# Earlier spectra, later weights: a reordered prologue and a longer pause in an FFT-and-MLP kernel

## The chip, the cores and the metric

The kernel runs on one core of a Trainium2 chip. The metric is the device time of one execution in microseconds (us). The engines are named as in the profile: PE (TensorE, matrix products; PEld its weight loads), DVE (VectorE), ACT (ScalarE), POOL (GpSimd) and SP (SyncE, which here only issues DMA transfers). PEclk is the share of its full clock that TensorE was granted.

## The reference

An input of 8 sequences of 3008 positions by 256 channels goes through a spectral layer and then through a two-layer MLP of 24064 tokens:

```python
X = np.fft.rfft(x, axis=1)                  # x: (8, 3008, 256), 3008 = 47 * 64
Yr = Xr @ w_r - Xi @ w_i + b_r
Yi = Xr @ w_i + Xi @ w_r + b_i
Y = soft_threshold(Yr, 0.01) + 1j * soft_threshold(Yi, 0.01)
y = np.fft.irfft(Y, n=3008, axis=1)
x = y.reshape(8 * 3008, 256)
h = x @ w_in                                # w_in: (256, 2048)
g = np.maximum(0.01 * h, h)
out = g @ w_out                             # w_out: (2048, 256)
```

The MLP's two weight matrices come as float64, so the kernel has to make float32 parts of them itself.

## The kernel before, in words

**Images and stages.** Each of the 8 sequences ("images", b = 0 to 7) passes three stages. `fwd(b)` loads x in pieces of 120 x 512 (`xin`, L235 for b = 0, L238 for later images), folds them on DVE (L245, L246), multiplies by the DFT matrix `fa` on PE (by way of the helper at L78), copies the result from PSUM on ACT (L264) and writes it to a DRAM buffer `u_dram` (L267). `mid(b)` takes the frequencies in 12 pairs of rows j: it reads `u` back (L329), multiplies by the second DFT matrix `fb` (L343), copies and adds (`ef`, L347 and L348), applies the complex weights (`w`), adds the bias part `kc` (L376, L388), soft-thresholds (L391, L392), applies a sign (`zf`, L396 on ACT, L398 and L400), multiplies by `gb`, copies the result `v` (L418) and writes it to `v_dram` (L420). `inverse` reads `v_dram` back and turns it into tokens, and `moe` runs the MLP over 47 chunks of 512 tokens, each product in three float32r terms (high by high, high by low, low by high; L92 into `psh`, L576 into `pso`).

**What overlaps.** Image 0 goes through all its stages first, in plain float32: this is the prologue, some 130 us. From then on PE runs the MLP, and the spectral stages of image b + 1 are laid between its products by `Stream` objects: a stage is a generator that yields its cost, and a stream advances it to a given fraction of its total (`MID` and `FWD`). At the start of `mid(b)` for b > 0 the generator yields a pause of `6 * CS`, right after it has issued the reads of `u` for its first two pairs; the stream spends that share of its total on no instructions.

**Weights in the prologue.** `load_win(c, ...)` loads quarter c of w_in (two halves of 512 KB, L155) and `convert_win(c)` makes its float32 parts: ACT starts with L131 and L132, DVE works on them in L133 to L137 and L162 to L168, then ACT (L171) and DVE (L172) split into high and low parts, twelve DVE instructions in all. `load_weights` loads the spectral weights (L121) and combines them on DVE (L122, L123); `split_consts` splits these and the DFT matrices into high and low parts (ACT L112, DVE L113) for the images after the first. `load_wout` does for w_out, in eight pieces named `raw`, what the former do for w_in; its conversion goes on into the first MLP chunks.

**What sets the order.** Each engine runs its own instructions in a fixed order. A scheduler that is part of the framework chooses this order when the kernel is built, from the order of the code, the data dependences and `tc.issue_after(x)`, which lets nothing under it be issued before x. The lists `written`, `reads`, `turned` and `thresholded` collect instructions of the stages (the writes of `u_dram`, the reads of `u`, the first transforms' copies, the thresholds) for that use. Transfers issued by one engine are issued in that engine's order; a transfer waits for a slot that an earlier one frees.

Of the kernel before, what the change touches and what calls it, by code (L numbers as in the profile page):

```python
# [8 lines left out]
F32 = mybir.dt.float32  # L9
# [9 lines left out]
N1, N2, NK1 = 47, 64, 24  # L19
NG, NS = 5, 13  # L20
P = 128
# [9 lines left out]
def spectral_mlp_kernel(  # L31
# [17 lines left out]
    NB = x.shape[0]  # L49
# [8 lines left out]
    CS = 512  # L58
# [45 lines left out]
    def load_plain(name, src, shape):  # L104
        consts[name] = const.tile(shape, F32, name=name)
        sync.dma_start(consts[name], src)

    def split_consts():
        for name in ("wr", "wd", "wn", "gb", "fa0", "fa1"):
            w = consts[name + "32"][0]  # L110
            hi, lo = pair(name, list(w.shape))
            act.copy(hi, w)  # L112
            dve.tensor_sub(lo, w, hi.bitcast(F32))  # L113
# [32 lines left out]
    def load_win(c, queues, behind=None):  # L146
        if c % 2 == 0:
            tag = ("wout_hi", "wout_lo")[c // 2]
            raw = sb.tile([P, 2, NH * NIN, 2], U32, name="win_raw", tag=tag, bufs=1)
            win_raw.extend((raw[:, 0], raw[:, 1]))  # L150
        r = win_raw[c].rearrange("p (a f) w -> p a (f w)", a=NH)
        iv = w_in.bitcast(U32).rearrange("(a p) f -> p a f", p=P)[:, :, 2 * c * NIN:2 * (c + 1) * NIN]
        for a, q in enumerate(queues):
            with tc.issue_after(behind.ins) if behind is not None else nullcontext():
                q.dma_start(r[:, a], iv[:, a])  # L155
# [19 lines left out]
    def load_wout():  # L175

        n = CS // D
        ov = w_out.bitcast(U32).rearrange("(a p) f -> p a f", p=P)
        raws = []

        def load(early):
            k = len(raws)
            tag, bufs = ("gl", 2) if early else (("e", 1), ("z", 1))[k % 2]
            raw = sb.tile([P, CS, 2], U32, name="raw", tag=tag, bufs=bufs)
            with tc.issue_after(reads[13 if early else -1].ins):
                sync.dma_start(raw.rearrange("p (a f) w -> p a (f w)", a=n), ov[:, k * n:(k + 1) * n, :])
            raws.append(raw)

        for k in range(2):
            load(True)  # L190
        yield 1
        consts["wout"] = tuple(
            sb.tile([P, NF, D], F32R, name=f"wout_{p}", tag=f"wout_{p}", bufs=1) for p in ("hi", "lo"))
        for c in range(NF // n):
            a = sb.tile([P, CS], F32, name="cva", tag="zf", bufs=1)
            q = sb.tile([P, CS], F32, name="cvq", tag="u", bufs=3)
            float64_parts(raws[c], a, q)
            dh, dl = (w[:, c * n:(c + 1) * n, :] for w in consts["wout"])
            a, q = (t.rearrange("p (a f) -> p a f", a=n) for t in (a, q))
            act.copy(dh, a)  # L200
            dve.tensor_sub(a, a, dh.bitcast(F32))
            converted.append(dve.tensor_add(dl, a, q))
            yield 1
            while c >= 1 and len(raws) < min(c + 3, NF // n):
                load(False)
# [2 lines left out]
    u_dram = {}  # L208
    v_dram = {}

    reads, written, turned, turning, thresholded = [], [], [], [], []
    NX = -(-NS // 2)
    XT = [("gf", 2)] + [("gl", 2)] * 2 + [("gh", 2)] * 2 + [("yc", 2)] * 2
    XT1 = [("yc", 2)] * 2 + [("gf", 2), ("gh", 2), ("yl", 2), ("yh", 2), ("gh", 2)]
# [1 line left out]
    def fwd(b):  # L216
# [5 lines left out]
        def load(c):  # L222
            cols = slice(2 * c * D, min(2 * c + 2, NS) * D)
            n = cols.stop - cols.start
            if b < NPRE:
                tag, bufs = (XT, XT1)[b][c]
                x2 = sb.tile([PA, 2, 2 * D], F32, name="xin", tag=tag, bufs=bufs)
                x_t[c] = [x2[:, h, :n] for h in range(2)]
            else:
                x_t[c] = [  # L230
                    sb.tile([PA, 2 * D], F32, name=f"xin{h}", tag="uv"[h], bufs=3 - h)[:, :n] for h in range(2)
                ]
            for h, t in enumerate(x_t[c]):
                if b == 0:
                    (act if h else sync).dma_start(t, x[b, h, :, cols])  # L235
                else:
                    with tc.issue_after(reads[-1].ins):
                        sync.dma_start(t, x[b, h, :, cols])  # L238
# [73 lines left out]
    def mid(b):  # L312
# [49 lines left out]
        def proj(j):  # L362
# [31 lines left out]
            for i in range(2):  # L394
                s = slice(64 * i, 64 * (i + 1))
                act.copy(zf[:64, i, :], t[s, 0, :])  # L396
                if b == 0 and j == NPAIR - 1:
                    dve.tensor_scalar(zf[64:, i, :], t[s, 1, :], sign[s, NK1 + j:NK1 + j + 1], None, ALU.mult)  # L398
                else:
                    act.mul(zf[64:, i, :], t[s, 1, :], sign[s, NK1 + j:NK1 + j + 1])  # L400
            if b == 0:
                z_t[j] = (zf,)
                yield 6 * D
# [8 lines left out]
        def stage_g(j):  # L412
            pg = bank("psh", 4) if b < 1 else bank("psf", 2)
            last = products(pg, [(consts["gb" if b else "gb32"], tuple(flat(z) for z in z_t.pop(j)))])
            if b == 0:
                turning.append(last)
            v = sb.tile([P, 2, D], F32, name="v", tag="v" if b else "y")
            act.copy(flat(v), pg)  # L418
            for c in range(2):
                act.dma_start(vd[c, 2 * j:2 * j + 2, :N2, :].rearrange("k n d -> n k d"), v[c * N2:(c + 1) * N2])  # L420

        for j in range(2):
            load(j)
        yield 6 * CS if b else 0
        if b:
            for s in range(NPAIR):
                if s + 2 < NPAIR:
# [225 lines left out]
    xs3 = sb.tile([PA, 3, 2 * D], F32, name="xs3", tag="yl")  # L653
    f0 = Stream(fwd(0), FWD)
    f0.to(0.01)
    load_win(0, (sync, act))
    load_plain("fb", fb, [P, NK1 + 1, N2])
    load_weights()
    brow = sb.tile([P, 2 * D], F32, name="brow", tag="kb", bufs=1)
    for p in (0, 32):  # L660
        for r, src in enumerate((b_r, b_i)):
            sync.dma_start(brow[p:p + 1, r * D:(r + 1) * D], src.unsqueeze(0))
    sign = const.tile([P, NK1 + NPAIR], F32, name="sign")
    sync.dma_start(sign, sg)
    sync.dma_start(consts["gb32"][0], gb)

    bo = sb.tile([P, 2 * D + P], F32R, name="bz", tag="t", bufs=1)
    bz, ones = bo[:, :2 * D], bo[:, 2 * D:]
    dve.memset(ones.bitcast(F32), 1.0)
    dve.memset(bz.bitcast(F32), 0.0)  # L670
    f0.finish()
    load_win(1, (sync, sync), written[7])
    pair("win", [P, 7, NQ, P])
    win_tmp = (
        sb.tile([P, NH * NIN], F32, name="cva", tag="vin"), sb.tile([P, NH * NIN], F32, name="cvq", tag="gf"),
        sb.tile([P, 4, 2, P], F32, name="ws", tag="yh"))
    act.copy(bz[:1], brow[:1])
    act.copy(bz[32:33], brow[32:33])
    dve.tensor_sub(bz[32:33], brow[32:33], bz[32:33].bitcast(F32))
    act.mul(fa32[:, 2], fa32[:, 1], -1.0)  # L680
    convert_win(0)
    with tc.issue_after(turned[0].ins):
        split_consts()
    m0 = Stream(mid(0), MID)
    m0.to(0.001)
    for c in range(2, 4):
        load_win(c, (sync, sync), reads[3])
    bias = const.tile([P, 2, D], F32, name="bias")
    with tc.issue_after(reads[3].ins):
        load_plain("ga", ga, [PA, 2, P])  # L690
        for r, src in enumerate((b_r, b_i)):
            sync.dma_start(bias[:, r, :], src.unsqueeze(0).broadcast_to([P, D]))
    fp = Stream(fwd(1), FWD)
    with tc.issue_after(turned[0].ins):
        convert_win(1)
    wout = load_wout()
    for i in range(1, 17):
        m0.to(i / 16)
        if i in (3, 8):
            convert_win(2 + i // 8)  # L700
        if 5 <= i < 12:
            next(fp.gen)
        if i == 13:
            next(wout)
# [10 lines left out]
    next(wout)  # L715


    mids = [Stream(mid(b), MID + 6 * CS) for b in range(1, NB)]
    cur, streams = -1, ()
    for i, pos in enumerate(moe()):  # L720
        if i % 2 == 0 and len(converted) < NQ:
# [121 lines left out]
```

## Time and profile before

| what | us |
|---|---|
| runs of the kernel before | 2603.67, 2605.85, 2608.62 |
| median | 2605.85 |
| profiled execution, its own time | 2600.34 |
| span of the profiled execution | 2598.6 |

The profiled execution is one more execution, 5.5 us below the median of the other three; 1.7 us of its time lie outside the span. Mean granted clock over the span: 0.993. In the profile a row of the windows view gives, for a stretch of time, the busy time of each engine with its number of instructions in parentheses. A row of the timeline gives the start, the time, the engine, the line, and the tiles "out<-in"; consecutive like instructions are one row with a count, and what an engine waited for before an instruction stands in brackets. "SPq" and "ACTq" rows are transfers being issued, not being carried out. Engines run side by side, so busy times do not add up to the span.

### The profile page before, as it was taken

How to read it: one execution, taken by the hardware profiler on the slowest of the kernel's cores; microseconds unless marked ns; L12 is line 12 of the kernel's file. 1: busy time of each engine (PE TensorE's matmuls, PEld its weight loads, DVE VectorE, ACT ScalarE, POOL GpSimd, SP SyncE). 2: the span in 40 equal slices, each digit the busy share in tenths (PEclk: the TensorE clock that was granted, in tenths of full speed). 3: DMA queues.
4: the chain of work that ended last, by engine and by line, in shares of the span. 5: the costliest groups of instructions: out<-in, count | busy, mean ns of one | idle time of the engine just before them, and what ended most of it. 6: DMA issues, size and time to landing. Idle time of an engine off the chain costs nothing.

```text
span 2598.6 us, 42643 instructions
## 1 busy us (share of the span) xinstructions
PE 2537.5 (98%) x16300; PEld 2281.5 (88%) x16300; DVE 1897.1 (73%) x3403; ACT 1668.5 (64%) x3174; POOL 229.6 (9%) x180
## 2 busy tenths in 40 slices
PE   5999999999999999999999999999999999999999
PEld 4689888999889998899988999889998889999998
DVE  7687786776777778777786777877777777767675
ACT  5766665776556666567665666566666667655564
POOL 0001121100110001100021000210002000000000
PEclk8999999999999999999999999999999999999999
DMA  8621132111221113211132111321113221101000
GB/s 259 179 85 50 48 89 72 54 47 48 82 78 49 45 41 90 75 55 51 33 97 68 49 49 37 104 67 49 49 36 101 64 58 48 44 17 32 9 17 17
DMA packets 119912, 165.13 MB, mean 64 GB/s; under 512 B 13601, under 2 KB 69917, under 8 KB 119709
## 3 DMA queue, kind: packets, MB, share of 16 engines
q1 hardware_dynamic: 79120, 115.55, 14.6%
q10 hardware_dynamic: 40589, 46.87, 7.1%
q8 instruction: 128, 2.10, 0.4%
q14 instruction: 75, 0.61, 0.1%
HBM read 86.60 MB, written 75.76 MB: 62 GB/s over the span
## 4 chain that ended last, share of the span: by engine, by line
PE 89%; DVE 3%; DMA 2%; ACT 1%; issue 0%; ACTq 0%; SPq 0%; DVEq 0%
PE pso L576 38%; PE psh L92 34%; PE psf L78 11%; PE psf L480 3%; PE psf L343 3%; DMA u<-u_dram 1%; DMA u_dram<-xin 1%; DVE yl L506 0%; DVE gl L563 0%; DMA raw<-w_out_dram 0%; DVE gf L557 0%; ACT gh L561 0%; DVE yt L511 0%; ACT gf L559 0%; DVE yc L512 0%
## 5 line engine op out<-in xcount | busy, mean ns | idle before, releaser
L92 PE MATMUL psh<-yh,win_hi 128*128 128x256 f32 x2632 | 752.3, 286 | 13.8 <-DVE gf L546 10.6
L92 PE MATMUL psh<-yl,win_hi 128*128 128x256 f32 x2632 | 738.3, 280 | 0.6 <-DVE yl L506 0.5
L92 PE MATMUL psh<-yh,win_lo 128*128 128x256 f32 x2632 | 737.9, 280 | 0.0
L576 PE MATMUL pso<-gh,wout_hi 128*128 128x512 f32 x1504 | 593.9, 395 | 0.0
L576 PE MATMUL pso<-gl,wout_hi 128*128 128x512 f32 x1504 | 591.1, 393 | 0.5 <-DVE gl L563 0.5
L576 PE MATMUL pso<-gh,wout_lo 128*128 128x512 f32 x1504 | 590.4, 393 | 0.0
L563 DVE TENSOR_TENSOR gl<-gf,gh 128x1024 fp32r<-128x1024 f32 x376 | 471.8, 1255 | 92.7 <-ACT gh L561 90.6
L92 PEld LDWEIGHTS psh<-yh,win_hi 128*128 128x128 f32 x2632 | 497.0, 189 | 30.7 <-DVE gf L546 15.4
L92 PEld LDWEIGHTS psh<-yl,win_hi 128*128 128x128 f32 x2632 | 497.0, 189 | 12.5 <-DVE yl L506 1.0
L92 PEld LDWEIGHTS psh<-yh,win_lo 128*128 128x128 f32 x2632 | 496.6, 189 | 0.2
L557 DVE TENSOR_TENSOR gf<-psh,u 128x512 f32<-128x512 f32 x376 | 259.1, 689 | 256.3 <-PE psh L92 255.1
L561 ACT CAST gh<-gf 128x1024 fp32r<-128x1024 f32 x376 | 396.4, 1054 | 7.1
L559 ACT ACTIVATE gf<-gf 128x768 f32<-128x768 f32 x376 | 320.0, 851 | 49.5 <-DVE gf L557 47.7
L576 PEld LDWEIGHTS pso<-gl,wout_hi 128*128 128x128 f32 x1504 | 282.5, 188 | 62.9 <-DVE gl L563 1.0
L576 PEld LDWEIGHTS pso<-gh,wout_hi 128*128 128x128 f32 x1504 | 283.1, 188 | 46.9 <-ACT gh L561 0.4
L576 PEld LDWEIGHTS pso<-gh,wout_lo 128*128 128x128 f32 x1504 | 282.9, 188 | 44.9
L556 ACT ACTIVATE gf<-psh 128x256 f32<-128x256 f32 x376 | 145.5, 387 | 266.6 <-PE psh L92 246.9
L542 ACT COPY p<-psh 128x256 f32<-128x256 f32 x376 | 140.1, 373 | 220.2 <-PE psh L92 219.1
L379 POOL TENSOR_TENSOR kb<-bias,kc 128x512 f32<-128x512 f32 x84 | 119.0, 1417 | 1530.6 <-ACT kc L376 1409.6
L543 DVE TENSOR_TENSOR u<-psh,p 128x256 f32<-128x256 f32 x376 | 158.6, 422 | 105.8 <-ACT p L542 103.5
L545 DVE TENSOR_TENSOR gf<-psh,u 128x256 f32<-128x256 f32 x376 | 159.3, 424 | 29.7 <-PE psh L92 2.0
L546 DVE TENSOR_TENSOR gf<-psh,gf 128x256 f32<-128x256 f32 x376 | 159.1, 423 | 9.0
(134 smaller groups left out, 3253.2 us busy)
## 6 DMA issues: line engine op xcount, KB each, us to landing
u<-u_dram SPq DMA_DIRECT2D x192, 128.0 KB, 2.7
v_dram<-v ACTq DMA_DIRECT2D x192, 128.0 KB, 2.4
out_dram<-ob SPq DMA_DIRECT2D x94, 256.0 KB, 2.1
vin<-v_dram SPq DMA_DIRECT2D x96, 240.0 KB, 3.5
xin<-x_dram SPq DMA_DIRECT2D x90, 240.0 KB, 3.0
u_dram<-xin ACTq DMA_DIRECT2D x72, 240.0 KB, 2.4
u_dram<-xin SPq DMA_DIRECT2D x24, 240.0 KB, 3.9
raw<-w_out_dram SPq DMA_DIRECT2D x8, 512.0 KB, 5.0
```

Of the source, the lines that this page charges most:

```text
L78: last = nc.tensor.matmul(dst, a, b, start=(i == 0), stop=(i == len(terms) - 1))
L92: mlp[:] = [nc.tensor.matmul(dst, a, b, start=start and i == 0, stop=i == 2, skip_group_check=True)]
L542: act.copy(p1, b1[:, lo])
L543: dve.tensor_add(u2, b1[:, hi], p1)
L545: dve.tensor_add(g[:, 3], b2[:, hi], u2)
L546: dve.tensor_add(g[:, 3], b2[:, lo], g[:, 3])
L556: act.activation(g[:, 0], b1[:, lo], AF.Prelu, alpha=SLOPE)
L557: dve.tensor_add(g[:, 1:3], b2.rearrange("p (k n) -> p k n", k=2), u2.unsqueeze(1).broadcast_to([P, 2, HT]))
L559: act.activation(g[:, 1:4], g[:, 1:4], AF.Prelu, alpha=SLOPE)
L561: cp = act.copy(gh, g)
L563: parted[:] = [cp, dve.tensor_sub(gl, g, gh.bitcast(F32))]
L576: mlp[:] = [nc.tensor.matmul(po, a[:, f, s], r[:, i], start=(f == 0 and j == 0), stop=(f == NF - 1 and j == 2),)]
```

## The change

Three things are different. (1) The pause of `mid(b)` for b > 0 is `9 * CS` instead of `6 * CS`, and the stream's total is enlarged by as much. (2) In the prologue, transfers and conversions stand in another order: both halves of w_in's quarter 0 are issued by SP after the last x load on SP; only 5 of the 25 columns of `fb` are loaded early, the other 20 after the first reads of `u`; the spectral weights and `gb` are loaded after the last write of `u_dram`; quarter 1 is loaded after the first reads of `u`, quarters 2 and 3 later inside `mid(0)`; `convert_win(0)` is issued after all of stage A's copies; the other three conversions and `split_consts` stand at steps 1, 4, 9 and 6 of the 16 steps of `mid(0)`; the first two loads of w_out stand behind the last reads instead of the 14th. (3) The writes of `v_dram` of image 0 are issued by SP instead of ACT.

```diff
--- before.py
+++ after.py
@@ -182,7 +182,7 @@
             k = len(raws)
             tag, bufs = ("gl", 2) if early else (("e", 1), ("z", 1))[k % 2]
             raw = sb.tile([P, CS, 2], U32, name="raw", tag=tag, bufs=bufs)
-            with tc.issue_after(reads[13 if early else -1].ins):
+            with tc.issue_after(reads[-1].ins):
                 sync.dma_start(raw.rearrange("p (a f) w -> p a (f w)", a=n), ov[:, k * n:(k + 1) * n, :])
             raws.append(raw)
 
@@ -208,7 +208,7 @@
     u_dram = {}
     v_dram = {}
 
-    reads, written, turned, turning, thresholded = [], [], [], [], []
+    reads, written, turned, turning, thresholded, signed, xload = [], [], [], [], [], [], []
     NX = -(-NS // 2)
     XT = [("gf", 2)] + [("gl", 2)] * 2 + [("gh", 2)] * 2 + [("yc", 2)] * 2
     XT1 = [("yc", 2)] * 2 + [("gf", 2), ("gh", 2), ("yl", 2), ("yh", 2), ("gh", 2)]
@@ -232,7 +232,9 @@
                 ]
             for h, t in enumerate(x_t[c]):
                 if b == 0:
-                    (act if h else sync).dma_start(t, x[b, h, :, cols])
+                    ld = (act if h else sync).dma_start(t, x[b, h, :, cols])
+                    if not h:
+                        xload[:] = [ld]
                 else:
                     with tc.issue_after(reads[-1].ins):
                         sync.dma_start(t, x[b, h, :, cols])
@@ -397,7 +399,7 @@
                 if b == 0 and j == NPAIR - 1:
                     dve.tensor_scalar(zf[64:, i, :], t[s, 1, :], sign[s, NK1 + j:NK1 + j + 1], None, ALU.mult)
                 else:
-                    act.mul(zf[64:, i, :], t[s, 1, :], sign[s, NK1 + j:NK1 + j + 1])
+                    signed[:] = [act.mul(zf[64:, i, :], t[s, 1, :], sign[s, NK1 + j:NK1 + j + 1])]
             if b == 0:
                 z_t[j] = (zf,)
                 yield 6 * D
@@ -417,11 +419,12 @@
             v = sb.tile([P, 2, D], F32, name="v", tag="v" if b else "y")
             act.copy(flat(v), pg)
             for c in range(2):
-                act.dma_start(vd[c, 2 * j:2 * j + 2, :N2, :].rearrange("k n d -> n k d"), v[c * N2:(c + 1) * N2])
+                (act if b else sync).dma_start(
+                    vd[c, 2 * j:2 * j + 2, :N2, :].rearrange("k n d -> n k d"), v[c * N2:(c + 1) * N2])
 
         for j in range(2):
             load(j)
-        yield 6 * CS if b else 0
+        yield 9 * CS if b else 0
         if b:
             for s in range(NPAIR):
                 if s + 2 < NPAIR:
@@ -653,51 +656,55 @@
     xs3 = sb.tile([PA, 3, 2 * D], F32, name="xs3", tag="yl")
     f0 = Stream(fwd(0), FWD)
     f0.to(0.01)
-    load_win(0, (sync, act))
-    load_plain("fb", fb, [P, NK1 + 1, N2])
-    load_weights()
+    load_win(0, (sync, sync), xload[0])
+    consts["fb"] = const.tile([P, NK1 + 1, N2], F32, name="fb")
+    sync.dma_start(consts["fb"][:, :5], fb[:, :5])
     brow = sb.tile([P, 2 * D], F32, name="brow", tag="kb", bufs=1)
     for p in (0, 32):
         for r, src in enumerate((b_r, b_i)):
             sync.dma_start(brow[p:p + 1, r * D:(r + 1) * D], src.unsqueeze(0))
     sign = const.tile([P, NK1 + NPAIR], F32, name="sign")
     sync.dma_start(sign, sg)
-    sync.dma_start(consts["gb32"][0], gb)
 
     bo = sb.tile([P, 2 * D + P], F32R, name="bz", tag="t", bufs=1)
     bz, ones = bo[:, :2 * D], bo[:, 2 * D:]
     dve.memset(ones.bitcast(F32), 1.0)
     dve.memset(bz.bitcast(F32), 0.0)
     f0.finish()
-    load_win(1, (sync, sync), written[7])
+    with tc.issue_after(written[-1].ins):
+        load_weights()
+        sync.dma_start(consts["gb32"][0], gb)
     pair("win", [P, 7, NQ, P])
     win_tmp = (
         sb.tile([P, NH * NIN], F32, name="cva", tag="vin"), sb.tile([P, NH * NIN], F32, name="cvq", tag="gf"),
         sb.tile([P, 4, 2, P], F32, name="ws", tag="yh"))
-    act.copy(bz[:1], brow[:1])
-    act.copy(bz[32:33], brow[32:33])
+    with tc.issue_after(turned[0].ins):
+        act.copy(bz[:1], brow[:1])
+        act.copy(bz[32:33], brow[32:33])
+        act.mul(fa32[:, 2], fa32[:, 1], -1.0)
+        convert_win(0)
     dve.tensor_sub(bz[32:33], brow[32:33], bz[32:33].bitcast(F32))
-    act.mul(fa32[:, 2], fa32[:, 1], -1.0)
-    convert_win(0)
-    with tc.issue_after(turned[0].ins):
-        split_consts()
     m0 = Stream(mid(0), MID)
     m0.to(0.001)
-    for c in range(2, 4):
-        load_win(c, (sync, sync), reads[3])
+    with tc.issue_after(reads[3].ins):
+        sync.dma_start(consts["fb"][:, 5:], fb[:, 5:])
+    load_win(1, (sync, sync), reads[3])
     bias = const.tile([P, 2, D], F32, name="bias")
     with tc.issue_after(reads[3].ins):
         load_plain("ga", ga, [PA, 2, P])
         for r, src in enumerate((b_r, b_i)):
             sync.dma_start(bias[:, r, :], src.unsqueeze(0).broadcast_to([P, D]))
     fp = Stream(fwd(1), FWD)
-    with tc.issue_after(turned[0].ins):
-        convert_win(1)
     wout = load_wout()
     for i in range(1, 17):
         m0.to(i / 16)
-        if i in (3, 8):
-            convert_win(2 + i // 8)
+        if i in (1, 4):
+            load_win(2 + i // 4, (sync, sync), reads[-1])
+        if i in (1, 4, 9):
+            convert_win(1 + i // 4)
+        if i == 6:
+            with tc.issue_after(thresholded[-1].ins), tc.issue_after(signed[-1].ins):
+                split_consts()
         if 5 <= i < 12:
             next(fp.gen)
         if i == 13:
@@ -715,7 +722,7 @@
     next(wout)
 
 
-    mids = [Stream(mid(b), MID + 6 * CS) for b in range(1, NB)]
+    mids = [Stream(mid(b), MID + 9 * CS) for b in range(1, NB)]
     cur, streams = -1, ()
     for i, pos in enumerate(moe()):
         if i % 2 == 0 and len(converted) < NQ:
```

In the order of SP's instructions (transfers only; names are out<-in, and "x7" is a run of like instructions), this stands at the beginning of the program in the kernel before:

```order
L155 DMA win_raw<-w_in_dram 128x1024
L267 DMA u_dram<-xin 120x512
L106 DMA fb<-fb_dram 128x1600
L121 DMA w_105<-w_r_dram 128x2x256
L121 DMA w_i<-w_i_dram 128x2x256
```

and further on, around the writes of `u_dram`:

```order
L665 DMA w_105<-gb_dram 128x128
L267 DMA u_dram<-xin 120x512 x7
L155 DMA win_raw<-w_in_dram 128x1024
L267 DMA u_dram<-xin 120x512 x3
L155 DMA win_raw<-w_in_dram 128x1024
L267 DMA u_dram<-xin 120x512
L267 DMA u_dram<-xin 120x256 x2
L329 DMA u<-u_dram 64x2x256 x6
L155 DMA win_raw<-w_in_dram 128x1024 x4
```

In the changed kernel SP has, from the second half of quarter 0 on:

```order
L155 DMA win_raw<-w_in_dram 128x1024
L661 DMA fb<-fb_dram 128x320
...
L269 DMA u_dram<-xin 120x512 x11
L269 DMA u_dram<-xin 120x256 x2
L121 DMA w_177<-w_r_dram 128x2x256
L121 DMA w_i<-w_i_dram 128x2x256
L676 DMA w_177<-gb_dram 128x128
L331 DMA u<-u_dram 64x2x256 x6
L690 DMA fb<-fb_dram 128x1280
L155 DMA win_raw<-w_in_dram 128x1024 x2
```

Quarter 1 (two instructions of L155) has gone from between the writes of `u_dram` to behind the first six reads of `u`; 1280 of the 1600 columns of `fb` have gone there too; the spectral weights now stand between the last write and the first read.

On DVE, the first additions of `mid(0)` (`ef`, L348) stand in the kernel before behind all of quarter 0 and beside quarter 1, whose first four instructions are already over:

```order
L172 TENSOR_TENSOR win_lo<-ws,win_hi 128x4x256
L133 TENSOR_SCALAR cva<-cva 128x1024
L134 TENSOR_SCALAR cva<-cva 128x1024
L135 SCALAR_TENSOR_TENSOR cva<-win_raw,cva 128x1024
L136 TENSOR_SCALAR win_raw<-cva 128x1024
L348 TENSOR_TENSOR ef<-ef 128x2x128
L137 TENSOR_TENSOR cvq<-cvq,win_raw 128x1024
L348 TENSOR_TENSOR ef<-ef 128x2x128
L162 TENSOR_TENSOR cva<-cva,cvq 128x1024
```

and in the changed kernel beside quarter 0:

```order
L136 TENSOR_SCALAR win_raw<-cva 128x1024
L137 TENSOR_TENSOR cvq<-cvq,win_raw 128x1024
L350 TENSOR_TENSOR ef<-ef 128x2x128
L162 TENSOR_TENSOR cva<-cva,cvq 128x1024
L350 TENSOR_TENSOR ef<-ef 128x2x128
L165 TENSOR_TENSOR ws<-cva 128x256
L166 TENSOR_TENSOR ws<-cva 128x256
L172 TENSOR_TENSOR win_lo<-cva,win_hi 128x2x256
L167 TENSOR_TENSOR ws<-ws,cva 128x256
```

So the whole of quarter 1, the last seven of quarter 0's twelve instructions and the six of `split_consts` (further on) now stand between the instructions of `mid(0)`.

On ACT, the end of `mid(0)` reads in the kernel before

```order
L318 DMA v_dram<-zero 48x256
L418 COPY v<-psh 128x512
L420 DMA v_dram<-v 64x2x256 x2
L418 COPY v<-psh 128x512
L396 COPY zf<-t 64x256 x2
L420 DMA v_dram<-v 64x2x256 x2
L418 COPY v<-psh 128x512
```

and in the changed kernel

```order
L320 DMA v_dram<-zero 48x256
L420 COPY v<-psh 128x512 x2
L398 COPY zf<-t 64x256 x2
L420 COPY v<-psh 128x512
```

with no writes of `v` between the copies.

## Rows read from the trace of the kernel before

**Rows 1.** Windows: PE, PEld, DVE, ACT, POOL busy (count), PEclk, DMA share, GB/s

```profile
16.00:20.00 4.00, 2.29 (x6) 0.72 (x4) 2.08 (x5) 2.35 (x3) 0.00 (x0) 1.00 1.00 397
...
50.00:80.00 30.00, 28.90 (x150) 23.35 (x150) 28.09 (x48) 24.03 (x50) 0.00 (x0) 1.00 0.80 236
...
80.00:97.00 17.00, 17.00 (x89) 13.92 (x88) 10.97 (x22) 15.25 (x32) 0.30 (x1) 1.00 0.35 93
...
168.00:2598.00 2430.00, 2404.71 (x15704) 2185.63 (x15704) 1771.97 (x3174) 1560.41 (x2966) 228.73 (x174) 1.00 0.19 55
```

**Rows 2.** Timeline of PE between stage A and mid(0)

```profile
20.30 1.12 PE L78 MATMUL psh<-xs,fa 120*120 120x512 f32 x2 [2.01 <-ACT xin L264]
...
22.55 0.59 PE L78 MATMUL psh<-xin,fa 120*120 120x256 f32 x2
...
39.91 5.86 PE L343 MATMUL psh<-fb,u 128*128 128x128 f32 x24 [16.76 <-DMA u<-u_dram]
```

**Rows 3.** Timeline of SP's queue: transfers issued (start us, us of issuing)

```profile
25.63 0.53 SPq L155 DMA_DIRECT2D win_raw<-w_in_dram  x1
...
28.27 1.94 SPq L155 DMA_DIRECT2D win_raw<-w_in_dram  x1
...
30.30 1.41 SPq L267 DMA_DIRECT2D u_dram<-xin  x3
...
36.38 3.94 SPq L329 DMA_DIRECT2D u<-u_dram  x6
```

**Rows 4.** DMA view, 0:36.3 us: packets; issues, KB each, us to landing

```profile
DMA packets 5672, 10.08 MB, mean 278 GB/s; under 512 B 981, under 2 KB 2152, under 8 KB 5672
...
win_raw<-w_in_dram SPq DMA_DIRECT2D x3, 512.0 KB, 5.6
...
fb<-fb_dram SPq DMA_DIRECT2D x1, 800.0 KB, 6.8
...
w<-w_r_dram SPq DMA_DIRECT2D x1, 256.0 KB, 5.8
...
w<-gb_dram SPq DMA_DIRECT2D x1, 64.0 KB, 2.0
```

**Rows 5.** Timeline of ACT: quarter 0's first conversion, inside stage A

```profile
17.65 1.14 ACT L131 ACTIVATE cvq<-win_raw 128x1024 f32<-128x1024 uint32 x1 [2.17 <-DMA win_raw<-w_in_dram]
```

**Rows 6.** Windows, instructions on tile cva alone, DVE, then ACT where listed

```profile
27.90:34.50 6.60, 3.59 (x7) 0.50 0.89 300
...
36.00:105.00 69.00, 20.99 (x33) 6.21 (x9) 0.92 0.65 187
```

**Rows 7.** Timeline of DVE: L113, L172 and L137 of the conversions

```profile
29.12 0.69 DVE L113 TENSOR_TENSOR wn_lo<-w,wn_hi 128x512 fp32r<-128x512 f32 x1
...
33.20 1.23 DVE L172 TENSOR_TENSOR win_lo<-ws,win_hi 128x1024 fp32r<-128x1024 f32 x1 [1.11 <-ACT win_hi L171]
...
42.95 1.22 DVE L137 TENSOR_TENSOR cvq<-cvq,win_raw 128x1024 f32<-128x1024 f32 x1
```

**Rows 8.** Windows: the whole of mid(0), from its first ef addition

```profile
42.60:102.60 60.00, 55.96 (x277) 45.12 (x276) 48.28 (x85) 47.05 (x94) 0.30 (x1) 0.97 0.66 194
```

**Rows 9.** Timeline of ACT: the end of mid(0)

```profile
101.77 0.59 ACT L418 COPY v<-psh 128x512 f32<-128x512 f32 x1 [1.41 <-issue]
...
102.39 0.41 ACT L396 COPY zf<-t 64x256 f32<-64x256 f32 x1
```

**Rows 10.** Waits of PE, 168:2598 us: us in total, times, longest

```profile
PE psf L343 <- DMA u<-u_dram: 9.6, 6, 2.4
```

**Rows 11.** Timeline: DVE and POOL in a stretch of the body

```profile
664.57 2.00 POOL L245 TENSOR_TENSOR xs<-xin,xin 120x512 f32<-120x512 f32 x1 [9.65 <-DMA xin<-x_dram]
...
665.32 1.52 DVE L511 TENSOR_TENSOR yt<-yc,yt 128x256 f32<-128x256 f32 x1
```

**Rows 12.** All of DVE's line L511: duration ns min/median/max

```profile
L511 DVE TENSOR_TENSOR yt<-yc,yt x47: 412/420/1521, 127.1 to 2519.7; 128x256 f32<-128x256 f32 x47
```

**Rows 13.** Windows, as in group 1, just after that stretch

```profile
667.00:673.00 6.00, 1.31 (x7) 1.04 (x7) 5.33 (x10) 3.80 (x8) 0.97 (x1) 0.79 0.00 0
```

## The prediction, made before the changed kernel ran

> **What bounds the kernel now.** The windows view, read first, splits the span in two: a body of 2430 us, in which PE is busy 2404.7 us, 99% [rows 1], and a prologue of some 168 us. In the body only PE's own idle time can be won, 25.3 us by the same row, and the view of PE's waits shows what of it has a name: the largest is 9.6 us in six waits for reads of `u`, where an image passes from `fwd` to `mid` [rows 10]. The prologue is looser. PE's timeline has one long hole: the last matmul of stage A begins at 22.55, the first `fb` product of `mid(0)` at 39.91, after 16.76 us of waiting for `u` [rows 2]. Those reads are issued by SP at 36.38 and later; ahead of them SP's queue still has writes of `u_dram`, the last at 30.30, and between the writes two halves of w_in's quarter 1, at 25.63 and 28.27 [rows 3]. The DMA view says what the transfers were doing up to there: 10.08 MB at a mean of 278 GB/s [rows 4], and inside it 397 GB/s in the stretch from 16 to 20 us [rows 1]. So the hole is a queue of bytes, not a computation. Behind it `mid(0)` is bound more tightly: in the 60 us from its first addition PE is busy 56.0 and DVE 48.3 [rows 8], and between 50 and 80 us DVE is busy 28.1 of 30 [rows 1].
>
> **Part 1, the queue ahead of the reads of `u`.** Moved behind the reads: two halves of 512 KB of quarter 1, and 20 of 25 columns of `fb`, 640 of 800 KB [rows 4], together 1664 KB. The two spectral weights of 256 KB and `gb` of 64 KB (the same rows) move behind the writes but stay ahead of the reads in the order. What a read of `u` waits for is the last write's landing, so these 576 KB no longer delay the writes; I count them as gone, though they share the wires for the 2 us before the reads. In all 2240 KB, 2.29 MB. At the mean rate while transfers ran, 10.08 MB in about 34.4 us or 293 GB/s, that is 7.8 us; at the 397 GB/s of the best stretch it is 5.8 us. The packets removed are of the kinds that ran in the fast stretch as well as in the slow ones, so I take the middle, **-6.8 us**: the reads at about 29.6, the first `fb` product, 3.5 us behind them as now, at about 33.1. A second brake also goes: ACT waited 2.17 us for quarter 0 inside stage A [rows 5] and PE 2.01 us for ACT's copy behind it [rows 2]; that lies inside the time the bytes take and is not counted again. Pushed to 33.1 the start is still well behind the last matmul of stage A, so PE's work there does not take over.
>
> By the Trainium skill ("DMA: Bandwidth & Descriptors", Issuing engines are not separate DMA queues), transfers started by any engine run on the same 16 DMA engines, and a second issuer saves only issue time. [...]
>
> **Part 2, what `mid(0)` takes on.** On DVE, one quarter costs 9.4 us of busy time: 20.99/3 on tile `cva` [rows 6], and the two steps that don't touch that tile, 1.22 and 1.23 [rows 7]. Before, `mid(0)` held quarter 1 from L137 on, 1.22 + 3.59 + 1.23 = 6.0 (the seven `cva` steps in the first row of [rows 6]). Now it holds quarter 0 from L162 on, 3.59 + 1.23 = 4.8, all of quarter 1, 9.4, and `split_consts`, six steps of which the wide ones take 0.69 [rows 7]: three wide, two of some 0.25 and one of 0.28 by their smaller tiles, an estimate of 2.8. So DVE gets 4.8 + 9.4 + 2.8 - 6.0 = 11.0 us more: 48.3 + 11.0 = 59.3 in a stretch of 60 [rows 8]. If DVE packs perfectly, nothing is added. If it reaches only the 94% of its busiest stretch (28.09 of 30, [rows 1]), the stretch takes 63.4 us, +3.4; at 90% it takes 65.9, +5.9. For packing speaks that before, DVE was busy only 11.0 of 17 us between 80 and 97 [rows 1], where the new work can lie. I take the middle of the first two, **+1.7 us**, and keep 0 and +5.9 as bounds. The loads of quarters 1 to 3 and of w_out come later, but each has tens of us to its use; were one late, ACT's L131 would stand still with `kc` and `zf` behind it, which is in the slower rival below.
>
> **Part 3, writes of `v` on SP.** At the end of `mid(0)` ACT's copy of `v` stood 1.41 us behind issues of earlier writes, and the last `zf` at 102.39 directly behind that copy [rows 9]; the new order has no issues there. The copy still waits its turn behind a 0.59 us predecessor, so I count **-0.6 us**, bounds 0 and -1.4. Behind the writes on SP stand only reads for later stages.
>
> The Trainium skill speaks against this part (same page, Queues, rings and completion order): each DMA engine takes turns between the queues that have work, so a write on ACT's row overtakes a backlog on SP's, and on SP's row it would have to wait behind it. No run shows `v`'s writes on SP. What it could cost is small here, as a rival: the loads seen at 5.6 to 6.8 us to landing [rows 4] would be the delay, and the buffer of `v` is wanted again a pair or two later, 5 us a pair by the 60 us of [rows 8]; only the last write is on the path, +2 us, the total then -3.7, chance 3 in 100, counted under "no change".
>
> **Part 4, the pause.** It moves no instruction of PE at the junction in a way that adds distance: between the last first-transform product of an image and its first `fb` product PE has the same 25 rows in both orders. So the 9.6 us of waits [rows 10] stay, **0 us**, with bounds -9.6 (all gone) and +2 (one more wait like the longest, 2.4).
>
> **Part 5, the body's order.** It is shuffled throughout, since the totals of the streams change. One accident shows what that can do: at 664.57 POOL runs two additions on `xin`, and DVE's L511 beside them takes 1.52 us [rows 11] where its median is 0.42 [rows 12]; PE is then busy only 1.31 us of the 6 after 667 [rows 13], 4.7 us lost. One such accident more or fewer is ±4.7; I take **0**.
>
> **Sum.** -6.8 + 1.7 - 0.6 + 0 + 0 = -5.7 us on the profiled execution, whose own time is 2600.3 us (span 2598.6 and 1.7 outside it): 2594.6. That execution lies 5.5 us below the median of the runs shown, 2605.85, which is what I predict against: **2600.2 us**. About 0.2%, 5.2 us, is what a measurement of this kernel can tell from no change, so the likeliest case lies close to that border.
>
> **The rivals.**
> First, `mid(0)` becomes DVE-bound: 94 to 90% packing, +3.4 to +5.9 us, total -4.0 to -1.5, 2601.9 to 2604.4 us. The 28.1 of 30 between 50 and 80 us speaks for it, the idle DVE between 80 and 97 against it [rows 1].
> Second, the hole is not set by bytes alone: writes of `u` wait for a free slot and for each landing, and SP's writes come in bursts [rows 3]. If only the bytes of quarter 1, 1.05 MB, shorten it, at 293 GB/s, the gain is 3.6, the total -2.5, 2603.4 us.
> Third, the pause or the shuffle does work in the body: an accident gone gives -10.4, all junction waits gone -15.3, so 2595.5 to 2590.6 us. For it speaks that the waits are there, against it the unchanged rows.
> Fourth, slower: each quarter goes back and forth between ACT and DVE (L131, L132; L133 to L168; L171; L172). Alone, quarter 0 took from 17.65 [rows 5] to 34.43, when the L172 at 33.20 ends [rows 7]: 16.8 us for 9.4 us of DVE's work, 7.4 us of handing over. In `mid(0)` each hand-over can hold up `ef` or `zf` behind it in its engine's fixed order. Two and a half quarters' worth uncovered is +18, total -6.8 + 18 - 0.6 = +10.6, 2616.5 us. It decides for slower once `mid(0)` grows by more than 7.4 + 5.2 = 12.6 us. Against it: before, quarters 2 and 3 ran inside `mid(0)` with PE at 96 to 100% from 50 to 97 us [rows 1].
>
> **How the numbers follow.** Chances: the forecast 0.48 (it straddles the border, 0.33 faster and 0.15 no change); DVE-bound 0.20 (0.18 no change, 0.02 slower); fewer bytes that count, with the rule on queues, 0.08 (0.07 no change, 0.01 faster); the body's gain 0.13, all faster; slower 0.11. Together faster 0.47, no change 0.40, slower 0.13. The range from 2592 to 2609 us holds the first three wholly and most of the body's gain, and leaves out the slower case and the far end of the gain.
>
> **What would show it.** Right: SP's first read of `u` near 29.6 instead of 36.38 and the first `fb` product near 33; `mid(0)` from its first addition to its last `zf` 60 to 63 us long with DVE busy over 90% of it; no issue time ahead of ACT's last copies of `v`; six waits for `u` in the body of the same 9 to 10 us. Wrong: reads of `u` that start no more than 4 us earlier, a `mid(0)` of over 66 us, PE waiting for ACT's `ef` or `kc` behind an L131, or a changed sum of waits in the body.

## The result, and the profile after

| | median us (12 runs each) | lowest to highest |
|---|---|---|
| before | 2601.59 | 2600.03 to 2608.62 |
| changed | 2610.6 | 2606.15 to 2616.47 |

The ratio is 1.0030, with a 95% interval of 1.0023 to 1.0038: slower by some 8 us, where 5.7 us less had been forecast. The forecast started from 2605.85 us, the median of three runs; over twelve runs the kernel before takes 2601.59, 4.3 us less. Line numbers of the changed kernel lie 2 to 3 above those of before (L345 for L343, L509 for L506). The profiled execution of the changed kernel has a span of 2610.2 us. Its windows view, with the columns of [rows 1], begins like this; the second row has no counterpart there, so the same stretch of before follows.

```profile
16.00:20.00 4.00, 4.00 (x13) 1.88 (x11) 2.00 (x4) 2.84 (x6) 0.00 (x0) 1.00 0.94 340
22.00:50.00 28.00, 14.82 (x77) 13.56 (x78) 17.42 (x28) 9.38 (x16) 0.00 (x0) 0.76 0.88 272
50.00:80.00 30.00, 26.06 (x133) 20.41 (x132) 26.80 (x51) 27.30 (x56) 0.00 (x0) 1.00 0.83 231
80.00:97.00 17.00, 14.98 (x75) 12.03 (x74) 14.03 (x25) 13.17 (x30) 0.00 (x0) 1.00 0.38 112
168.00:2598.00 2430.00, 2406.77 (x15691) 2186.42 (x15690) 1761.82 (x3175) 1552.54 (x2964) 232.83 (x174) 1.00 0.19 54
```

The kernel before, windows view:

```profile
22.00:50.00 28.00, 11.18 (x50) 9.87 (x49) 20.69 (x36) 13.63 (x25) 0.00 (x0) 0.63 0.84 263
```

Stage A now runs without a gap (PE 4.00 of 4 between 16 and 20 us). In 22 to 50 us PE does 3.6 us more, but DVE 3.3 us less and ACT 4.3 us less. In 50 to 80 us the picture is turned round: PE falls from 28.9 to 26.1, ACT rises from 24.0 to 27.3. The start of `mid(0)`, changed kernel, SP's queue and then PE's timeline:

```profile
27.59 0.40 SPq L121 DMA_DIRECT2D w<-w_r_dram  x1
...
29.56 3.94 SPq L331 DMA_DIRECT2D u<-u_dram  x6
```

```profile
34.03 3.75 PE L345 MATMUL psh<-fb,u 128*128 128x128 f32 x16 [13.70 <-DMA u<-u_dram]
...
87.17 1.13 PE L78 MATMUL psh<-zf,w 128*128 128x512 f32 x2 [2.02 <-ACT zf L402]
...
101.01 1.13 PE L78 MATMUL psh<-zf,w 128*128 128x512 f32 x2 [2.57 <-ACT zf L402]
...
103.66 2.08 PE L78 MATMUL psh<-zf,w 128*128 128x512 f32 x2 [1.52 <-ACT zf L398]
```

The first read of `u` is issued at 29.56 (forecast 29.6; before 36.38, [rows 3]), the first `fb` product starts at 34.03 (before 39.91, [rows 2]), 5.9 us earlier. But the last `zf` product starts at 103.66; in the trace before it stood at 103.26. So, against that trace, all of the gain is gone within `mid(0)`; against the mean of four that is given below, 2.4 of 7.1 us are left. In the changed kernel DVE and ACT have more to do there. Windows view from the first `ef` addition to the end of the last `zf`, changed kernel and then before:

```profile
36.73:103.60 66.87, 55.73 (x275) 44.05 (x274) 57.05 (x103) 52.88 (x106) 0.30 (x1) 0.98 0.68 193
```

```profile
42.61:103.21 60.60, 55.95 (x277) 45.10 (x276) 48.28 (x85) 47.64 (x95) 0.30 (x1) 0.97 0.66 193
```

One of the places where PE waits is seen in ACT's timeline, changed kernel:

```profile
84.39 0.69 ACT L131 ACTIVATE cvq<-raw 128x512 f32<-128x512 uint32 x1 [3.18 <-DMA raw<-w_out_dram]
84.98 0.35 ACT L378 COPY kc<-pso 128x256 f32<-128x256 f32 x1
85.23 0.40 ACT L398 COPY zf<-t 64x256 f32<-64x256 f32 x1
```

ACT stands 3.18 us for the first piece of w_out, whose load now goes out at 78.47 instead of 55.76; `kc` and `zf` are behind it in ACT's order, and PE's wait at 87.17 is for them. The waits of PE in the body, changed kernel, the four largest of eight, in the form of [rows 10]:

```profile
PE psf L345 <- DMA u<-u_dram: 8.0, 6, 1.6
PE psh L92 <- DVE gf L549: 5.6, 7, 1.9
PE psf L78 <- ACT eh L360: 3.1, 3, 1.8
PE psh L92 <- DVE yl L509: 2.3, 2, 1.4
```

The six waits for `u` are still six, 8.0 us instead of 9.6; others for `eh` and `yl` are larger. All eight add up to 23.0 us, those of before to 21.8, so these waits alone do not make the loss.

Single executions vary in the prologue. Three profiles of kernels that differ from before only in the pause (the experiments below) have the same order there on every engine, and their first reads of `u` are at 37.24, 37.55 and 38.91, their last `zf` products at 105.89 to 108.44, their first MLP products at 126.60 to 130.16 (before: 36.38, 103.26, 123.96). The trace on which the prediction rested was the fastest of the four up to there. For comparisons below, their mean is used: reads 37.5, first `fb` product 41.1, last `zf` 106.1, first MLP product 127.3, start of the last conversion step of w_out (L202) 179.3.

### The profile page after: what moved, and what is told of

Its sections match the earlier page's. It is cut to its first block, busy times and chain, and to the rows that moved or that the text cites. A ratio compares the mean times of both kernels' runs of the same rounds, so it can differ in the third digit from the quotient of the medians.

```text
span 2610.2 us, 42629 instructions
## 1 busy us (share of the span) xinstructions
PE 2544.0 (97%) x16300; PEld 2284.6 (88%) x16300; DVE 1886.6 (72%) x3403; ACT 1661.9 (64%) x3174; POOL 233.7 (9%) x180
## 4 chain that ended last, share of the span: by engine, by line
PE 87%; DVE 3%; ACT 2%; DMA 1%; issue 1%; POOL 0%; SPq 0%; ACTq 0%; DVEq 0%; POOLq 0%
PE pso L579 37%; PE psh L92 34%; PE psf L78 11%; PE psf L483 3%; PE psf L345 3%; DVE yl L509 1%; DMA u<-u_dram 1%; DMA u_dram<-xin 1%; DVE gl L566 0%; ACT gh L564 0%; ACT gf L562 0%; DVE gf L560 0%; ACT zf L402 0%; ACT yh L508 0%; DVE t L392 0%
## 5 line engine op out<-in xcount | busy, mean ns | idle before, releaser
L566 DVE TENSOR_TENSOR gl<-gf,gh 128x1024 fp32r<-128x1024 f32 x376 | 465.6, 1238 | 98.2 <-ACT gh L564 96.7
```

The lines of the kernel that those rows point to most:

```text
L566: parted[:] = [cp, dve.tensor_sub(gl, g, gh.bitcast(F32))]
```

## The experiments

Each was timed beside the kernel before, in 11 executions, the pause alone in 5; "ratio" is to before, with its 95% interval, and 0.0010 is 2.6 us. Two theories stood at the start: the prologue's part lost the time, or the body did, by the longer pause.

**The pause alone.**

```diff
-        yield 6 * CS if b else 0
+        yield 9 * CS if b else 0
-    mids = [Stream(mid(b), MID + 6 * CS) for b in range(1, NB)]
+    mids = [Stream(mid(b), MID + 9 * CS) for b in range(1, NB)]
```

> The kernel before with the pause of 9*CS alone, prologue untouched. Theory A (the body lost the larger part: a longer pause shifts the streams' shares, other instructions collide, and each PE stall is followed by a stretch at a lower clock): slower than before by 6 to 10 us. Theory B (the prologue alone lost it, the pause costs nothing, as predicted): within 2 us of before. Theory C (the pause gains at the junctions): faster by 3 to 10 us, with fewer than 9.6 us of waits for u.

Measured: 2610.83 us, ratio 1.0034 (1.0021 to 1.0046). Theory A: the pause alone costs as much as the whole change (its mechanism is looked at below).

**The prologue alone**, the changed kernel with `6 * CS`.

> The changed kernel with the pause back at 6*CS: the prologue's part of the change alone. The order of the prologue is that of the changed kernel up to the first MLP products. Theory A: slower than before by 0 to 4 us, the first MLP product at about 125.6 us as in the changed kernel, body as before. Theory B: slower by 8 to 10 us, like the changed kernel.

Measured: 2603.96 us, ratio 1.0009 (1.0000 to 1.0018); first MLP product at 125.64, exactly as in the changed kernel. Theory A again; the prologue's part is worth nothing or costs up to some 4.7 us. This kernel and the changed one differ in the pause alone, and by the medians the pause costs 6.6 us between them.

**Other pauses**, 3 and 12 times CS on the kernel before.

> The kernel before with a pause of 3*CS. Theory A1 (a longer pause squeezes the pairs of mid into less time, or takes distance away, so the cost grows with the pause): faster than before by 3 to 9 us. Theory A2 (the pause only shifts which instructions of the spectral stages fall beside which of the MLP, and what follows is luck of place): no such order; anything between 6 us faster and 10 us slower, with stalls of 1 to 3 us at other places than before, and those that trace of before and of this share at the same places unchanged.

> The kernel before with a pause of 12*CS. Theory A1: slower than before by 13 to 20 us, twice what 9*CS cost. Theory A2: not above 12 us, quite possibly nearer to before than 9*CS, with the groups of stalls near 465, 2117 and 2230 us of the 9*CS traces gone or elsewhere.

Measured: 3*CS 2605.59 us, ratio 1.0008 (0.9999 to 1.0017); 12*CS 2606.11, ratio 1.0016 (1.0007 to 1.0025). With 6*CS as 1 and 9*CS as 1.0034 there is no order by length; theory A1 falls. With 12*CS the waits for `u` do shrink, to 3.6 us in five (and one of 1.5 us whose end the profile puts to nothing), but those for `eh` grow from 1.8 to 5.9, and nothing is won. The stalls show what a new pause does. PE's timeline, changed kernel, at three places (the profile of the pause alone has the first wait at 467.44 and the third group at 2229.68):

```profile
465.32 0.39 PE L92 MATMUL psh<-yl,win_hi 128*128 128x256 f32 x1 [0.81 <-DVE yl L509]
...
467.39 0.38 PE L92 MATMUL psh<-yl,win_hi 128*128 128x256 f32 x1 [1.45 <-DVE yl L509]
...
2118.84 0.39 PE L78 MATMUL psf<-wr_hi,eh 128*128 128x256 f32 x1 [1.83 <-ACT eh L360]
...
2228.27 0.39 PE L92 MATMUL psh<-yh,win_hi 128*128 128x256 f32 x1 [1.30 <-DVE u L546]
2229.36 0.58 PE L78 MATMUL psf<-wr_hi,eh 128*128 128x256 f32 x1 [0.47 <-ACT eh L360]
2232.12 0.58 PE L78 MATMUL psf<-wn_hi,eh 128*128 128x256 f32 x1 [0.68 <-ACT v L420]
```

In before PE has no wait between 455 and 475 us, nor between 2226 and 2233. DVE's timeline, changed kernel, shows what it does there:

```profile
462.38 0.42 DVE L514 TENSOR_TENSOR yt<-yc,yt 128x256 f32<-128x256 f32 x1
462.71 0.42 DVE L515 TENSOR_TENSOR yc<-yc 128x256 f32<-128x256 f32 x1
463.05 0.69 DVE L509 TENSOR_TENSOR yl<-yc,yh 128x512 fp32r<-128x512 f32 x1
463.65 0.42 DVE L516 TENSOR_TENSOR yc<-yc,yt 128x256 f32<-128x256 f32 x1
463.98 0.69 DVE L392 TENSOR_TENSOR t<-psf,kb 128x512 f32<-128x512 f32 x1
464.58 0.68 DVE L509 TENSOR_TENSOR yl<-yt,yh 128x512 fp32r<-128x512 f32 x1
465.18 0.42 DVE L393 TENSOR_SCALAR c<-t 128x512 f32<-128x512 f32 x1
465.52 1.22 DVE L566 TENSOR_TENSOR gl<-gf,gh 128x1024 fp32r<-128x1024 f32 x1
466.65 0.68 DVE L509 TENSOR_TENSOR yl<-yc,yh 128x512 fp32r<-128x512 f32 x1
```

A threshold of `mid` (L392, L393) and the MLP's `gl` (L566) stand between the three `yl` on which PE's next products wait, with no gap. The threshold alone is 1.1 us there. With 3*CS, PE has instead one wait of 3.69 us for `eh` at 464.95; with 12*CS, none between 455 and 475. This is as A2 has it: the pause decides which steps of `mid` fall beside the making of a new chunk's tokens.

Not every such stall is in the total. From the start of w_out's last conversion step (L202) to the issue of the 72nd of the 94 writes of `out`, between 2083 and 2090 us, the changed kernel takes 1908.3 us and the pause alone 1907.0; before takes 1906.9, the prologue alone 1906.3, 12*CS 1909.2. What PE loses at 465 us it has regained by then. From the 79th write to the last all of them take 300.0 to 300.1. What stays lost arises between these two writes. Windows of that stretch for the changed kernel, the pause alone and the prologue alone:

```profile
2086.27:2307.16 220.89, 216.61 (x1409) 197.10 (x1408) 152.00 (x277) 142.48 (x277) 12.81 (x9) 0.98 0.15 42
```

```profile
2089.23:2305.87 216.64, 212.37 (x1409) 193.30 (x1408) 151.89 (x277) 142.38 (x277) 13.51 (x9) 1.00 0.15 43
```

```profile
2084.36:2297.03 212.67, 211.31 (x1409) 193.23 (x1408) 151.56 (x277) 142.59 (x277) 12.78 (x9) 1.00 0.15 44
```

Before takes 212.7 there as well, 3*CS 213.1, 12*CS 212.6. With 9*CS PE is idle 4.3 us instead of 1.4, by the waits at 2118 and 2228 to 2232 us shown above, and the pause alone needs 4.0 us more than the prologue alone. The further 4.3 us of the changed kernel go with a granted clock of 0.98 instead of 1.00. After such a stall the clock may fall; windows of the changed kernel, and of the pause alone at the same place:

```profile
2220.00:2230.00 10.00, 8.23 (x56) 7.20 (x55) 7.45 (x15) 8.52 (x19) 0.00 (x0) 0.97 0.01 2
2230.00:2240.00 10.00, 9.32 (x47) 8.18 (x47) 3.64 (x8) 2.91 (x5) 1.30 (x1) 0.69 0.11 26
```

```profile
2220.00:2230.00 10.00, 8.70 (x58) 7.63 (x57) 7.39 (x16) 7.51 (x17) 0.00 (x0) 1.00 0.01 2
2230.00:2240.00 10.00, 8.86 (x58) 7.69 (x57) 6.32 (x12) 3.93 (x8) 1.29 (x1) 1.00 0.11 26
```

In the first, the granted clock is 0.69 over 10 us, and 47 matmuls are done where 58 are with the clock at 1.00: the same stalls cost more in one execution than in another. From the start of w_out's last step (L202) to the end of the span, ten profiles with 6*CS take 2421.8 to 2424.3 us, whatever their prologue; 3*CS 2423.2, 12*CS 2425.0, the pause alone 2426.7, the changed kernel 2432.3. So the traces put some 4 to 9 us of 9*CS into the body; the timings say 5 to 12. The pause alone was timed 8.9 us slower, but its one trace has only 4 of that in the body: it also reached the last L202 at 182.3, late for an order of the prologue that it shares with three others (175.7, 178.8, 180.5). How the 8.9 us spread over its other executions is not shown.

**Two mends of the prologue**, both on the prologue alone: w_out's first loads behind the 14th read again, and `split_consts` ahead of `mid(0)` again.

```diff
-            with tc.issue_after(reads[-1].ins):
+            with tc.issue_after(reads[13 if early else -1].ins):
```

> As the prologue alone, but the first two loads of w_out stand behind the 14th read again instead of the last one. Only SP's order differs; PE, ACT and DVE have the same instructions in the same order. Theory W (ACT's L131 on the raw tile, 3.18 us late in the changed kernel at 84.39, holds zf and PE behind it): that wait is gone, the first MLP product 2 to 3 us earlier, the total 2 to 3 us less than the prologue alone. Theory D (DVE and ACT are simply full in mid(0), and the wait only moved idle time): the first MLP product moves by less than 1 us.

```diff
         convert_win(0)
+        split_consts()
...
-        if i == 6:
-            with tc.issue_after(thresholded[-1].ins), tc.issue_after(signed[-1].ins):
-                split_consts()
```

> As the prologue alone, but split_consts (five ACT casts, six DVE subtractions) stands ahead of mid(0) again, where PE waits for u anyway. Theory D (mid(0) is bound by the added work on DVE and ACT): mid(0) is 2 to 3 us shorter, the first MLP product 2 to 3 us earlier. Theory W (late loads and the hand-overs set it): less than 1 us.

> The prologue's part alone (6*CS) with both mends: w_out's first two loads behind the 14th read, split_consts ahead of mid(0). If the two costs are apart, their gains add: 6 to 7 us less than the prologue alone, 4 to 5 us faster than before, first MLP product near 120 us. If DVE's total work up to the end of w_out's conversion near 168 us is what counts (Theory T), the MLP starts near 120 us but the second chunk's end gains only 0 to 2 us on split_consts alone, and the total is within 1.5 us of it.

| | ratio | last zf product | first MLP product | last L202 |
|---|---|---|---|---|
| prologue alone | 1.0009 (1.0000 to 1.0018) | 103.88 | 125.64 | 178.1 |
| w_out early | 0.9997 (0.9988 to 1.0006) | 102.51 | 124.13 | 177.3 |
| split early | 0.9992 (0.9983 to 1.0000) | 99.72 | 121.50 | 172.4 |
| both | 0.9995 (0.9986 to 1.0004) | 100.64 | 123.76 | 173.6 |

Each mend is worth 3 to 4 us by the medians (2601.01 and 2600.08 against 2603.96), and each moves the end of `mid(0)`: theories W and D both have a part. The first MLP product came 1.5 us earlier with w_out early, where W had 2 to 3, and 4.1 earlier with the split early, where D had 2 to 3. Together the mends are worth no more than the second alone, and the first MLP product came at 123.76 instead of near 120: the gains do not add. Which wait takes the place of those removed was not followed.

**Single edits on the kernel before**: `fb` split in two (20 columns after the reads); quarter 1 loaded after the reads; and both ways of writing `v`.

```diff
-    load_plain("fb", fb, [P, NK1 + 1, N2])
+    sync.dma_start(consts["fb"][:, :5], fb[:, :5])
...
+        sync.dma_start(consts["fb"][:, 5:], fb[:, 5:])
```

> The kernel before with one edit of the change: 20 of fb's 25 columns are loaded after the first reads of u. Quarter 1 stays between the writes of u_dram, and its conversion and split_consts stay ahead of mid(0). Bytes moved: 0.66 MB. Theory T (what the change loses in the prologue is DVE's and ACT's work that it takes out of the hole): the reads of u start 2 to 3 us earlier, nothing is given back, the total is 1.5 to 3 us less than before. Theory U (any earlier start of mid(0) is given back, since the stretch up to 168 us is bound by DVE's total): total within 1 us of before.

```diff
-    load_win(1, (sync, sync), written[7])
-    for c in range(2, 4):
+    for c in range(1, 4):
         load_win(c, (sync, sync), reads[3])
```

> The kernel before with one other edit of the change: quarter 1 is loaded after the first reads of u, so that its conversion falls into mid(0). Bytes moved: 1.05 MB. The reads of u start some 3 to 4 us earlier by the bytes. Theory T: given back inside mid(0), first MLP product within 1.5 us of that of before, the total within 1.5 us of before or slower. Theory N (as predicted, mid(0) has room for this one quarter's 3.3 us of added DVE work): 2 to 4 us less than before.

Measured: `fb` split 2605.30 us, ratio 1.0013 (1.0005 to 1.0022); quarter 1 later 2601.52, ratio 0.9993 (0.9984 to 1.0002). SP's queue with `fb` split, and then with quarter 1 later:

```profile
27.62 3.85 SPq L267 DMA_DIRECT2D u_dram<-xin  x5
36.49 3.95 SPq L329 DMA_DIRECT2D u<-u_dram  x6
```

```profile
22.50 9.25 SPq L267 DMA_DIRECT2D u_dram<-xin  x13
33.60 4.01 SPq L329 DMA_DIRECT2D u<-u_dram  x6
```

The bytes of `fb` gave little or nothing: the reads stand at 36.49 (and at 36.62 in the run with `v` on SP below), 1 us ahead of the mean and within before's own 36.4 to 38.9; by the prediction's 293 GB/s it should have been 2.2 us. Those of quarter 1 gave 3.9 us against the mean. After the last write is issued (31.47 and 31.75) the reads follow in 5.0 us where quarter 1 is among the writes, in 1.9 us where it is not.

The run with quarter 1 later had gained 3.9 us at the `fb` product (37.23). DVE's busy time in 22 to 50 us is 15.97 there, 20.69 in before, so work is taken out of the hole, PE's long wait for `u`. But against the mean 3.5 us of the gain are still there at the last `zf` product (102.55) and 3.6 at the first MLP product (123.64): `mid(0)` had room for this one quarter, as theory N says. At the last L202 (178.1) 1.2 us are left, and the total is told neither from before nor from 2 us less, so between T and N it does not decide.

Neither theory held for `fb` split: it is slower than before. The reason stays open; its trace has a wait of 2.4 us for a read of `u` at 79 us that before has not.

```diff
-                act.dma_start(vd[c, 2 * j:2 * j + 2, :N2, :].rearrange("k n d -> n k d"), ...
+                (act if b else sync).dma_start(vd[c, 2 * j:2 * j + 2, :N2, :] ...
```

> The prologue's part alone (6*CS), with the writes of v of image 0 issued by ACT again. Theory P (as predicted, issues ahead of the last copies hold zf): last zf product and first MLP product 0 to 1.4 us later than in the prologue alone, the total 0 to 1.5 us more. Theory Q (with ACT at 91% busy between 50 and 80 us, 24 issues of some 0.6 us each count in the middle of mid(0) as well): 3 us or more later. Theory R (SP's queue delays the writes): earlier.

> As the run with fb split alone, and with the writes of v of image 0 issued by SP, as in the change. Theory P: -0.6 us against that run, by the last v copies alone (bounds 0 and -1.4). Theory Q (24 issues of some 0.6 us weigh on ACT all through mid(0)): 2 to 4 us less than that run, first MLP product 2 to 4 us earlier. Theory R: slower.

> The kernel before with the writes of v of image 0 issued by SP and nothing else. Theory P (as predicted, only the last copies of mid(0) gain): 0 to 1.4 us less than before, not to be told from no change. Theory Q (the issues weigh on ACT all through mid(0), as the pair of runs with fb split suggests): 3 to 6 us less, first MLP product 3 us or more earlier than the 127 us that is the mean of the four profiles with before's prologue. Theory R (SP's queue delays the writes): slower.

Measured, `v` written by SP against by ACT: in the changed prologue 2603.96 against 2605.02 (ratios 1.0009 and 1.0015, not told apart); with `fb` split 2599.81 against 2605.30 (0.9990, 0.9981 to 0.9999, and 1.0013); alone on before 2608.14 (1.0020, 1.0011 to 1.0029). The same edit is a gain, nothing or a loss by what stands around it: in the first within theory P, in the second more than theory Q said, in the third as theory R says. With ACT issuing in the changed prologue the trace has the last `zf` product at 106.28 instead of 103.88 and the first MLP product at 130.13 instead of 125.64, as theory Q says, and with SP alone on before they stand at 109.95 and 132.68; but these two traces are each of the slowest of 11 executions. No theory held in all three, and the cause of the loss stays open. The run with `fb` split and `v` on SP is the one that beats both kernels, by some 2.6 us over before, barely clear of it.

## Why the prediction was wrong

**The step that failed is the pause's zero.** "It moves no instruction of PE at the junction in a way that adds distance" was right, the six waits took 8.0 us after 9.6, and it was the wrong place to look: the pause changes the stream's total, and with it where all of `mid` lies beside the MLP. Part 5 did name this effect, but priced it as one accident of 4.7 us either way around nothing, and did not ask how many of the some 15 us of other waits in the body could grow; the rivals had the shuffle only as a gain. Measured: +8.9 us by the ratio (5.5 to 12), shown by that edit alone. In the traces 4 us of it are a few stalls in one stretch of the last image, and up to 4.3 more a lower clock in the same stretch. That it would be a loss and not a gain could not have been read from the trace of before; that the spread could be larger than ±4.7 could, from those 15 us.

**Part 1 was right in its result, partly wrong in its cause.** Reads at 29.56 against 29.6, first `fb` product 34.03 against 33.1; the closeness is in part luck. Not every byte counted alike: `fb` gave at most some 1 us, and quarter 1, among the writes, gave 3.9. The remaining 3 to 4 us go with an earlier end of stage A (the main run of writes of `u_dram` starts at 17.90, with quarter 1 later at 22.50). Behind that may stand the stall of [rows 5], which Part 1 took to lie inside the bytes' time, or the spectral weights; no run takes either alone. By the Trainium skill ("DMA: Bandwidth & Descriptors", Issuing engines are not separate DMA queues), transfers started by any engine run on the same 16 DMA engines and interleave. The run with quarter 1 later agrees, 1.9 us instead of 5.0 from the last write's issue to the first read; the run with `fb` split, whose bytes stood further ahead of the writes, shows no gain clear of the spread.

**Part 2 was mis-sized.** `mid(0)`, from first `fb` product to last `zf` product, took 69.6 us; before, 63.4 in the trace of [rows 2], 65.0 on the mean. That is +4.6 to +6.3 instead of +1.7, around the upper bound of 5.9. DVE's work was counted somewhat too high: it grew by 8.8 us, from 48.3 to 57.1, where 11.0 had been added. What failed is the packing: 57.1 of 66.9 us is 85%, below the lower bound of 90%. Left out was ACT's work: quarter 0's three L171, quarter 1's L131 and L132 and the six L112 of `split_consts` go into `mid(0)` too, and ACT went from 47.6 to 52.9 us busy there, between 50 and 80 us from 24.0 to 27.3 of 30. With `split_consts` ahead of `mid(0)` again it took 65.5 us (34.20 to 99.72) instead of the 70.0 of the prologue alone, so that one move makes most of the growth. "Each has tens of us to its use" was wrong for w_out: its load at 78.47 was 3.18 us late for an L131 that had kept its early place in ACT's order. And "the hole is a queue of bytes, not a computation" missed that DVE used it: in before DVE is busy 20.7 of 28 us from 22 to 50, and from 22 us to the last L202 it does 121.0 us of work in before, 121.5 in the changed kernel. What is not done in the hole is done later. For `split_consts` the runs show that DVE and ACT then hold PE; for quarter 1 they do not.

**Part 3** was seen (no issues ahead of ACT's last copies), its price unresolved. "Behind the writes on SP stand only reads for later stages" was wrong: in the changed kernel SP issues writes of `v` at 55.76 and 58.91, and reads of `u` for the same `mid(0)` behind them at 58.21 and 60.19. Whether that costs anything is not shown. **The rivals:** the slower one was named with hand-overs inside `mid(0)` and +18 us; the end was slower, but by another mechanism, and `mid(0)` alone would not have made it so: the prologue's part measured 1.0009.

## What to carry to other kernels

A stretch in which PE waits for a transfer may be where another engine earns its keep: before emptying it, add up, for every engine, the work that leaves it and ask where that is done instead, and whether there is room. If a load is moved later, look where the first instruction that waits for it stands in its engine's order, and what stands behind it. A parameter that rescales an interleaving moves every later coincidence; its effect is a spread to be measured at several values, not a sum of moved instructions.

## What the runs showed of the hardware

The same stalls were followed by a granted clock of 0.69 over 10 us in one execution and 1.00 in another, and the stretch around them took 220.9 us in the first and 216.6 in the second. And in four executions of a prologue in one and the same order the first MLP product came at 123.96 to 130.16, a spread of 6 us, more than the change was forecast to bring. They ran on at least two chips; no run tells the chip from chance.
